# A fused gated attention and long-convolution kernel on one core: the order of all engines' tasks and their PSUM banks written out, with 81 places changed

## The chip, the core and the metric

One NeuronCore of a Trainium2 chip. Its engines run at the same time and meet through semaphores: TensorE (PE; its weight loads are shown as PEld), VectorE (DVE), ScalarE (ACT), GpSimd (POOL) and SyncE (SP). Each runs its own instructions strictly in order. SP, POOL and a little ACT issue transfers; 16 DMA engines carry them out. The metric is device microseconds of one execution; lower is better.

## The reference, cut to what matters

For each of 8 batches with S = 3136 rows:

```python
scores = (1/S) * z @ z.T                     # z: S x 64, symmetric
out    = maximum(scores, 0)**2 @ v           # v: S x 256
x      = u * out                             # S x 256
x1, x2, x3 = split(x @ w_proj, 3)            # 256 x 768
conv   = irfft(rfft(x2, axis=1) * rfft(filter))   # circular convolution over S
y      = (x1 * conv * x3) @ w_out            # float32, S x 256
```

## The kernel before, in words

**Attention.** The 3136 columns of a batch are cut into 7 chunks (512, five times, 256 and 320), the rows into tiles of 128. A unit (b, c, k) is a pair of row tiles of chunk c in batch b. TensorE computes its scores into a pair of PSUM banks (`score_mm`, matmuls that read zT_t). ACT or DVE takes the positive part into R_t (L1919 or L1921), and one of them squares it into A_t (L1928 or L1930). TensorE then weighs the rows of v with it, in two phases (matmuls that read A_t and v_t) and sums a chunk in one pair of banks. The scores are symmetric, so part of them isn't computed twice: SP issues DMA transposes of A_t into M_t, M2e_t or M2o_t (L1848), from which later chunks are weighed. A_t has 8 buffers, and a buffer is free only when its transposes have landed; M_t, M2e_t and M2o_t have one buffer each.

**From a chunk to the spectrum.** When a chunk's sum is done, DVE multiplies it with uT_t into xT_t (L1975). TensorE projects xT_t (matmuls with wp), ACT or DVE takes x1 out of PSUM (x_t), DVE multiplies it with x3 into gate_t (L1256). x2 goes through the first step of a long transform (`dft1`), is taken out as s_t and put to a scratch in HBM (spec<-s_t, L1028 and L1031). At the end of a batch eight frequency groups g = 0 to 7 follow, two to a load: SP loads spec_in_t (L1062), TensorE transforms, the result xh is multiplied with the filter's spectrum H on DVE (L1357, L1361, L1362), TensorE transforms back, the result goes to gs_t (two buffers) and back to the scratch (spec<-gs_t, L1406). Then, chunk by chunk, conv_in_t is loaded, transformed, multiplied with gate_t into yT_t (L1462), multiplied with w_out (matmuls with wo), taken out as ost_t (two buffers) and stored (out_dram<-ost_t, L1511). These steps of batch b run among the attention of batch b+1. The last batch's are split finer (`load_parts`, L1077), and three of the chunks of batch 6 are held back to fill the end, with their loads into v_t's space.

**Loads.** POOL casts u, v and z from HBM to bf16 (un_t, v_t, zn_t). DVE doubles z into zd_t (L1613), SP transposes it into zT_t (L1620), in four pieces per batch; the scores of a batch need all four. SP also transposes u into uT_t (L1565).

**The order.** The builder makes 5,477 tasks, each with an engine (or two to choose from), dependences, buffers and a cost. `Plan.go` puts them in an order by a replay on costs and then emits their instructions in this order, so it fixes each engine's queue. TensorE follows the string `ORDER`, one letter for a kind of work (S scores, w and v the two phases of a weighing, A and B and Z queues of other matmuls, Q the frequency groups), and takes within a kind the task that is ready first (`pick_pe`). ACT, DVE, SP and POOL take the ready task with the earliest start (`pick`); `ENGINES` names the engine where there is a choice. Of the four pairs of banks a task takes the one that came free first (`Pairs.take`). Where TensorE would idle near the end, `fill` puts in matmuls of the identity that keep it busy. All of this happens on the host while the program is built; on the chip an instruction waits only for what it needs and for the instructions before it on its engine.

Of the kernel before, what the change touches and what calls it, by code (L numbers as in the profile page):

```python
# [11 lines left out]
P = 128  # L12
# [10 lines left out]
INF = float("inf")  # L23
# [17 lines left out]
SPARE = 0.25  # L41
TURN = 0.235
# [14 lines left out]
    "vwSSwQwQAvAvSAvvwSAvwvSvwwwSvvQwwwSvSQvwAvQAvASvAQwwvSwvQwASAwvSwSwSvwASvSAwvAwSAvSwwwAvvASAvvAvvSSw"
    "wwSAvSAwvvSvASwAwwSBSBvwvSAvASwBvSBvAwAwABvBAwSvSwvAwAvSAvwSwwABSBwSvvAwAASAvwBvSBwAwABSwBvSvvSvvSwB"
    "ABvAwwSvwSwSAvBwABvvvSSwAwASvBvwBSwwAvSASwvwvBSBvwvASwAwwASAvQwvSQwvvSvQwwSQvwQvwQvSAvBABwAwBSAvBvvw"
    "SvSwwAASAwAvSvQwSwQwvSQvvvQwBwBwASvASwvwvSwwSvQvvwwvQSwwBvwSvBSvAvASAwASwvSSvvwQwQAvAwwvSASvSAwAQAwS"  # L60
    "wwQwSvASAvvwSwvvvSSvwvwvvwSAwSwASvwSvvAwBASBvwSwvSSwBvABvABvBwBwSBvSwvSAvwAwwSAvSAwvAwSAvBvBSvwSvAAA"
    "wABSwBwBAwwwBAAvAAvASvSvvvBABwASwwSwASAAvvSAvwvSBvSwwSwBSwSvwvSvSAvAvBQBwAvQwAvwQvwSvSQwAwwQAvvSvwQQ"
    "wwSvwAQvSAwvSwSvBwvSBvwvSAwAvvQSwBwBwQwBQvBQvvSvQwSSvwASwAvSvAwwAAwwvAvSvwwAvvwSvSAwSvwSwvBSwBAvSwAS"
    "vQSvwvvASwASwwwSQvvAwSSAwvSvwASvvSwwQwAvASAvwvvSvwwSAwASvvvwSSAvwAwAwSBABvvBwBSBwvSAvBAvSwAwASvvSBwS"
    "BvwwBwABvASvvSAwAwSSwBwBAvAASwAwBvBAAAvABSwvBSvwSvvSSvwBvBwwAwAvSSwwvvwAAAwSAvwSAvASSvwwvwSSQvvBwBQv"
    "vBSvBwwSvwAwAvwSSvAwAQvQvwSvQAwBABQwwvSvSQwBvwBAQAvSvvAQAwwAwQAvwSSvSwwvSSwAvvvSwQAvQwvSwQwwBSvQBvvS"
    "wvwwAvSvvwSvwwSAvQvwQvwSSvwSvAwSASvwAwSSAwwAwSASwvwvSSwvAwAvSAvASwwAvAvSvvSvwwvSwSvAvvAwBSBwvBwSBBBv"
    "wSvSAvAwwSSvvwSwSBvBwAvASvwwwSwBvBSAvAvvwwSwAAAAAvASwvSASwvBABSvvwSAvASwwwSwvwvvwSvSwvSSAwABvwvSwBSv"
    "wwSwSvwSBvBBvvBSvwvwASvAvwSwSAwASvAvAvSwASAwAvAQwvQwBvSwBQAwAwSvQAvwAwwQvvQvwSvQwABwBAQvwSvSQvvSwwQw"
    "BvSBvQvvSwSwwwvSvvvwwSAvSvAwwwSQvSvvSAwAvwSAvASASAQwSwwwQvSwQvASwASwvvwSwAvASvvwQSwwvAvAvSvvwSwwSABw"  # L70
    "BAvSvvSABABAwAwSSvvSvwASwASvwBSwBvwAwSAvSvAvAvSwBvwSBwAwAwAwSBABvvSAwAvSAwABSBwBvSvwBSvvvwSAvAAwABvB"
# [75 lines left out]
class Pairs:  # L147
# [5 lines left out]
    def when(self, ahead=0):  # L153
        return sorted(self.freed)[ahead]
# [1915 lines left out]
```

## Time and profile before

| what | value |
|---|---|
| three runs, median | 948.25 us (946.97 to 950.78) |
| the profiled execution, first to last instruction | 944.1 us |
| TensorE busy | 914.1 us (97%) |
| DVE, ACT, POOL busy | 838.5, 819.7, 248.8 us |
| TensorE's granted clock, mean | 0.997 |
| DMA, mean over the span | 181 GB/s |
| longest waits of TensorE by the profile | 2.1 us for gate_t, 1.8 us for v_t, 1.6 us for M_t |

The profile has one execution. Busy times are unions of the instructions' spans; a busy TensorE need not be at its peak, since the ends of matmuls are modelled. A wait is idle time of an engine just before an instruction, put down to the event that came last. SP's instructions count as issues: their length is the time for which SP was held, and the transfer lands later. Transfers of one kind are named out<-in, as M_t<-A_t.

### The profile page before, as it was taken

Reading aid. Unit: us, or ns where it says so; the run is one execution under the profiler, and the core shown is the slowest. Engines: PE = TensorE matmul, PEld = TensorE weight load, DVE = VectorE, ACT = ScalarE, POOL = GpSimd, SP = SyncE. Lnnn points to the kernel's source line nnn. Section 1 sums busy time; section 2 is a strip of 40 time slices with the busy share of each in tenths; the row PEclk is TensorE's granted clock in tenths of the full one; section 3 lists DMA queues with packets and bytes.
Section 4 is the critical chain, followed back from the end, with each engine's and each line's share of the span. In section 5 each row is a group of like instructions: output and inputs, shape, how many; then the busy total and the mean of one; then the engine's idle time right before and its main releaser. Section 6 shows DMA issues by size and latency. Waiting matters only on the chain.

```text
span 944.1 us, 30298 instructions
## 1 busy us (share of the span) xinstructions
PE 914.1 (97%) x12423; PEld 557.1 (59%) x12423; DVE 838.5 (89%) x1116; ACT 819.7 (87%) x953; POOL 248.8 (26%) x585
## 2 busy tenths in 40 slices
PE   8999999999999999999999999999999999999986
PEld 3446565566555666556665665666665666666654
DVE  8987899998888998999888988989988999899785
ACT  7968988999889988888989998889988999899573
POOL 5244223231322322223121321333123140101030
PEclk9999999999999999999999999999999999999999
DMA  9999799978999889998899989999889989897867
GB/s 155 162 181 181 117 179 184 181 150 182 170 217 201 146 181 192 209 156 159 190 183 215 176 155 200 173 184 174 183 172 207 221 138 196 193 216 132 193 189 241
DMA packets 331643, 170.70 MB, mean 181 GB/s; under 512 B 242886, under 2 KB 307142, under 8 KB 331504
## 3 DMA queue, kind: packets, MB, share of 16 engines
q1 hardware_dynamic: 301624, 131.98, 70.1%
q0 software_dynamic: 29168, 35.13, 26.4%
q8 instruction: 97, 1.59, 0.7%
q10 hardware_dynamic: 712, 1.66, 0.6%
q14 instruction: 42, 0.34, 0.1%
HBM read 90.26 MB, written 53.05 MB: 152 GB/s over the span
## 4 chain that ended last, share of the span: by engine, by line
PE 77%; DMA 10%; DVE 6%; ACT 3%; issue 2%; SPq 1%; POOL 0%; ACTq 0%; DVEq 0%; POOLq 0%
PE ps_s L516 77%; DMA M_t<-A_t 4%; DMA out_dram<-ost_t 1%; ACT R_t L1919 1%; DMA M_t<-spec_in_t 1%; DVE xh L1357 1%; ACT A_t L1928 1%; DVE yT_t L1462 1%; DVE A_t L1930 1%; DMA v_t<-spec 1%; DMA spec<-gs_t 1%; DMA M2e_t<-A_t 1%; ACT gs_t L582 1%; DVE R_t L1357 1%; DMA spec_in_t<-spec 0%
## 5 line engine op out<-in xcount | busy, mean ns | idle before, releaser
L516 PE MATMUL ps_s<-A_t,v_t 64*128 64x512 bf16 (+5 forms) x4766 | 516.1, 352 | 0.9 <-DVE A_t L1930 0.7
L516 PEld LDWEIGHTS <-v_t 64*128 64x128 bf16 (+1 forms) x6528 | 306.4, 98 | 187.7 <-PE ps_s L516 19.3
L1919 ACT ACTIVATE R_t<-ps_s 128x1024 f32<-128x1024 f32 (+3 forms) x359 | 336.9, 962 | 47.4 <-PE ps_s L516 43.8
L1928 ACT ACTIVATE A_t<-R_t 128x1024 bf16<-128x1024 f32 (+2 forms) x281 | 271.8, 993 | 15.3 <-DMA M_t<-A_t 6.3
L1930 DVE SCALAR_TENSOR_TENSOR A_t<-R_t 128x1024 bf16<-128x1024 f32 (+3 forms) x211 | 233.6, 1123 | 21.6 <-ACT R_t L1919 12.1
L516 PE MATMUL ps_s<-zT_t 64*128 64x512 bf16 (+5 forms) x1186 | 192.2, 351 | 3.6 <-DVE gate_t L1256 2.1
L1921 DVE TENSOR_SCALAR R_t<-ps_s 128x1024 f32<-128x1024 f32 (+4 forms) x153 | 170.2, 1123 | 20.9 <-PE ps_s L516 10.4
L639 POOL COPY tick<-A_t 1x1 bf16<-1x1 bf16 x159 | 56.2, 354 | 428.0 <-ACT A_t L1928 264.2
L516 PE MATMUL ps_s<-xT_t,wp 64*128 64x512 bf16 (+3 forms) x976 | 124.7, 352 | 0.1
L516 PE MATMUL ps_s<-M_t,v_t 64*128 64x512 bf16 (+4 forms) x860 | 97.2, 353 | 3.2 <-DMA M_t<-A_t 2.4
L516 PEld LDWEIGHTS <-zT_t 64*128 64x128 bf16 (+1 forms) x1219 | 69.1, 97 | 51.7 <-issue 8.2
L582 ACT ACTIVATE x_t<-ps_s 128x1024 bf16<-128x1024 f32 (+3 forms) x75 | 69.5, 928 | 22.8 <-PE ps_s L516 22.5
L1357 DVE TENSOR_TENSOR xh<-xh,H 128x1024 bf16<-128x1024 bf16 x120 | 81.7, 685 | 2.3 <-ACT xh L582 1.4
L1256 DVE TENSOR_TENSOR gate_t<-ps_s,x_t 128x512 bf16<-128x512 f32 (+2 forms) x112 | 64.4, 617 | 12.4 <-PE ps_s L516 9.0
L1462 DVE TENSOR_TENSOR yT_t<-ps_s,gate_t 128x1024 bf16<-128x1024 f32 (+2 forms) x53 | 56.9, 1078 | 14.3 <-PE ps_s L516 14.1
L1975 DVE TENSOR_TENSOR xT_t<-ps_s,uT_t 128x512 bf16<-128x512 f32 (+2 forms) x112 | 64.0, 613 | 6.3 <-PE ps_s L516 5.8
L516 PEld LDWEIGHTS <-wp 64*128 64x128 bf16 (+1 forms) x976 | 48.0, 96 | 29.7 <-PE ps_s L516 2.0
L516 PE MATMUL ps_s<-wp,xT_t 64*128 64x256 bf16 (+2 forms) x944 | 64.2, 266 | 0.8 <-ACT R_t L1919 0.7
L516 PE MATMUL ps_s<-wo,yT_t 64*128 64x256 bf16 (+2 forms) x904 | 62.1, 266 | 2.2 <-DVE yT_t L1462 1.0
L625 POOL DMA_DIRECT2D un_t<-in_u_dram x112 | 57.9, 518 | 17.4 <-issue 15.6
L651 POOL DMA_DIRECT2D v_t<-in_v_dram x112 | 58.2, 524 | 14.1 <-issue 10.4
L516 PEld LDWEIGHTS <-xT_t 64*128 64x128 bf16 (+1 forms) x944 | 44.1, 97 | 19.3 <-issue 1.5
(156 smaller groups left out, 905.7 us busy)
## 6 DMA issues: line engine op xcount, KB each, us to landing
out_dram<-ost_t SPq DMA_DIRECT2D x60, 256.0 KB
spec_in_t<-spec SPq DMA_DIRECT2D x56, 192.0 KB
spec<-gs_t SPq DMA_DIRECT2D x56, 192.0 KB
v_t<-in_v_dram POOLq DMA_DIRECT2D x80, 128.0 KB, 4.8
un_t<-in_u_dram POOLq DMA_DIRECT2D x80, 128.0 KB, 4.4
spec<-s_t SPq DMA_DIRECT2D x40, 256.0 KB
conv_in_t<-spec SPq DMA_DIRECT2D x34, 256.0 KB
out_dram<-ost_t SPq DMA_DIRECT2D x18, 128.0 KB
```

The costliest lines, as they stand in the source:

```text
L516: got = nc.tensor.matmul(o, *args, **kw)
L582: got = nc.scalar.activation(out_, in_, AF.Copy)
L625: nc.gpsimd.dma_start(out=t[ds(j * N1, N1), lo - t0 : hi - t0, :], in_=x[:, n2 : n2 + hi - lo, :])
L651: nc.gpsimd.dma_start(out=t[ds(j * N1, N1), ds(v_at(a), (b - a) * D)], in_=r[:, n2 + a - lo : n2 + b - lo, :].rearrange("p t d -> p (t d)"),)
L1256: has_read(nc.vector.tensor_tensor(o[:, :, ::-1] if h == 0 else o, p, x, ALU.mult), p)
L1357: nc.vector.tensor_tensor(x[:, 1 - i], x[:, 0], h, ALU.mult)
L1462: has_read(nc.vector.tensor_tensor(yb["y"][:, :, 0:w], p, gates[b, c][:, :, 0:w], ALU.mult), p)
L1919: has_read(nc.scalar.activation(r, p, AF.Relu), p)
L1921: has_read(nc.vector.tensor_single_scalar(r, p, 0.0, ALU.max), p)
L1928: nc.scalar.activation(a, r, AF.Square, scale=1.0 / float(S))
L1930: nc.vector.scalar_tensor_tensor(a, r, inv_s2, r, ALU.mult, ALU.mult)
L1975: has_read(nc.vector.tensor_tensor(x[:, :, ::-1] if h == 0 else x, f, ut, ALU.mult), f)
```

## The change

Before, a string of letters, a list of engines and the planner's own rules gave the order. After, the order itself is stored: `ORDER` holds two characters for each task, and `go` emits the tasks one after the other; `BANKS` holds the pair of banks of each task that takes one. Codes past the last task stand for the identity matmuls in one of the four pairs. `pick_pe`, `pick`, `offer` and the test in `fill` are gone; a task that is not ready when its turn comes makes the build fail. The tasks, their instructions, their dependences and buffers are the same, but for four tasks on another engine and for 10 identity groups in place of 12.

Against the order in which the kernel before issues, the stored one differs in 81 places, which were chosen on a replay of traced transfers. The codes can't be read by eye, so the differences that matter below are spelled out here (b is the batch; times are the starts in the profile before, to find them).

SP's queue:

| instruction | at, us | moved |
|---|---|---|
| spec<-s_t, b 3, first tiles | 374.83 | behind both M_t<-A_t that begin at 376.13 |
| spec_in_t<-spec, b 2, g 4 and 5 | 388.95 | ahead of M2e_t<-A_t (384.76) and out_dram<-ost_t (386.76); uT_t<-un_t (391.51) goes with it |
| M_t<-A_t, b 3, two of them | 399.80, 401.42 | the first directly behind the store of 386.76, then the load of 397.85, then the second, then the put of 394.55, M2o_t<-A_t of 404.64, the store of 392.89, zT_t of 407.21, spec<-s_t of 399.29 |
| out_dram<-ost_t, b 1; zT_t<-zd_t, b 4 | 416.68; 421.97 | eight and four places down |
| spec<-s_t, b 4, first tiles | 494.53 | behind both M_t<-A_t that begin at 495.41 |
| spec_in_t<-spec, b 3, g 4 and 5 | 504.18 | three places down |
| out_dram<-ost_t, b 2, last | 540.95 | nine places down |
| out_dram<-ost_t, b 3 | 617.19 | behind both M_t<-A_t that begin at 619.18 |
| zT_t<-zd_t, b 6, third piece | 624.99 | four places down, behind spec<-s_t of 633.19 |
| spec<-gs_t, b 4, first | 637.96 | ahead of the store of 633.78 and the load of 635.93 |
| spec_in_t<-spec, b 4, g 6 and 7 | 635.93 | behind M_t<-A_t of 640.81 |
| spec<-gs_t, b 4, second; zT_t<-zd_t, b 6, last piece | 643.16; 649.55 | behind the three M_t<-A_t that begin at 652.31, in this order |
| out_dram<-ost_t, b 3 | 647.47 | behind the put of 659.53 |
| spec<-gs_t, b 5, third | 760.35 | eight places down |
| spec_in_t<-spec, b 6, g 6 and 7 | 840.42 | five places down |
| spec_in_t<-spec, b 7, first half | 881.53 | behind the first two v_t<-spec (888.57, 889.13) |
| gs_t<-spec, b 7, the second pair | 886.88 | behind conv_in_t<-spec of 890.32 |

Some ten more move by one to three places. TensorE: 34 groups move by one to ten places, 16 of them in batch 0; among the others the weighing from M_t that begins at 504.81 (behind the groups at 505.24 and 505.68). Some 20 groups change places in their pair of banks; for most it follows from the move. DVE: the copy into zd_t at 620.65 moves behind the eviction xh<-ps_s at 624.78; four more tasks move by two to four places. ACT: six tasks swap with neighbours. POOL: two loads of v. A square in batch 0, one in batch 5 and an x1 eviction in batch 0 go from DVE to ACT, one positive part in batch 0 from ACT to DVE.

```diff
--- before.py
+++ after.py
 ORDER = (
-    "ASSAwSSvAwSSAwwSSvvwSBvwSvSwvSvwSwSvvSwSSvwwSvvwwSvwAvSwAwwSvSvSAvvwwSwwSvvvSABwvBwwSvvAwAvSSwwvSSwA"
...
+    "0G0H00010203130I170J1404050K1806150L190716080C1B091G0D1Crx1H0A1A0B1D1L1I1Q0E1M0O1F0F1K1R1N1V1Zry1Wrz"
...
 )
...
 ENGINES = (
...
-KINDS = {"A": "FA", "B": "FB", "Z": "FZ", "w": "W"}
+BANKS = (
+    "0123012312313213213213212301330130303102102102102021201213213131231210120210212010232132132132032032"
...
+)
+CODES = "0123456789ABCDEFGHIJKLMNOPQRSTUVWXYZabcdefghijklmnopqrstuvwxyz!#$%&()*+,-./:;<=>?@[]^_{|}~"
...
     def __init__(self, n):
         self.freed = [0.0] * n
 
-    def when(self, ahead=0):
-        return sorted(self.freed)[ahead]
-
-    def take(self, now=0.0):
-        k = min(range(len(self.freed)), key=lambda i: self.freed[i])
+    def take(self, k):
         self.freed[k] = INF
         return k
 
...
     def __init__(self):
         self.free = {e: 0.0 for e in ("PE", "ACT", "DVE", "SP", "POOL")}
         self.queues = {"S": [], "Q": [], "W": [], "FA": [], "FB": [], "FZ": []}
-        self.pend = {e: [] for e in ("ACT", "DVE", "SP", "POOL")}
         self.form = None
         self.flips = {}
...
         seen = {}
         for s in task.takes:
             k = seen.get(id(s), 0)
-            t = max(t, s.when(k))
+            t = max(t, s.freed[self.bank] if s is self.pairs else s.when(k))
             seen[id(s)] = k + 1
         return t
 
...
         return t + (a / f if a / f <= b / (1 - f) else a + b)
 
...
-        return best and (best[1], best[2], e)
-
-    def fill(self, until):
-        if self.queues["S"] or self.queues["W"] or not any(self.queues.values()):
-            return False
-        start = self.free["PE"]
-        if until < start + c_pe(512) + SPARE or self.pairs.when() > start:
-            return False
-        self.got = [(self.pairs, self.pairs.take(start))]
+
+    def fill(self, bank):
+        self.bank = bank
+        self.got = [(self.pairs, self.pairs.take(bank))]
         self.form = "H"
         self.filler()
-        self.free["PE"] = start + c_pe(512)
-        self.pairs.freed[self.got[0][1]] = self.free["PE"]
-        return True
+        self.free["PE"] += c_pe(512)
+        self.pairs.freed[bank] = self.free["PE"]
 
     def go(self):
+        every = self.tasks + [t.second for t in self.tasks if t.second]
         either = [t for t in self.tasks if t.kind is None and len(t.cost) > 1]
         assert len(either) == len(ENGINES)
         for task, e in zip(either, ENGINES):
             e = {"a": "ACT", "d": "DVE", "p": "POOL"}[e]
-            for x in task.cost:
-                if x != e and task in self.pend[x]:
-                    self.pend[x].remove(task)
             task.cost = {e: task.cost[e]}
-        while True:
-            got = []
-            x = self.pick_pe()
-            if x:
-                got.append((x[0], 0, x[1], "PE", x[2]))
-            for i, e in enumerate(self.pend):
-                x = self.pick(e)
-                if x:
-                    got.append((x[0], i + 1, x[1], e, None))
-            if not got:
-                break
-            start, _, task, e, k = min(got, key=lambda g: g[:2])
-            if self.fill(start):
+        n = len(CODES)
+        codes = [CODES.index(ORDER[i]) * n + CODES.index(ORDER[i + 1]) for i in range(0, len(ORDER), 2)]
+        kinds = [every[k].kind for k in codes if k < len(every) and every[k].kind]
+        banks = iter(BANKS)
+        at = 0
+        for k in codes:
+            if k >= len(every):
+                self.fill(k - len(every))
                 continue
-            if not k:
-                self.run(task, e, start)
-                continue
-            (self.rest if k == "v" else self.queues[KINDS.get(k, k)]).remove(task)
-            form = "F" if task.full else "Q" if k == "Q" else "H"
-            if form == "H" and self.form == "Q" and "Q" in ORDER[self.at + 1 : self.at + 1 + NEAR]:
-                form = "Q"
-            if self.form is not None and self.form != form:
-                start += FORM
-            self.form = form
-            if k in "wv":
-                flip, turned = self.flips.get(task.sum, (0, 0.0))
-                if k == "w":
-                    task.flip = flip
-                    task.second.flip = flip ^ 1
-                    self.rest.append(task.second)
-                elif flip != task.flip:
-                    start = max(start, turned + TURN)
-                self.flips[task.sum] = task.flip, start + task.cost["PE"]
-            for x in task.flips:
-                self.flips[x] = 0, start + task.cost["PE"]
-            self.at += 1
+            task = every[k]
+            (e,) = task.cost
+            assert task.end is None and not task.left
+            if self.pairs in task.takes:
+                self.bank = int(next(banks))
+            start = max(self.free[e], self.ready_at(task))
+            assert start < INF
+            if task.kind:
+                at += 1
+                form = "F" if task.full else "Q" if task.kind == "Q" else "H"
+                if form == "H" and self.form == "Q" and "Q" in kinds[at : at + NEAR]:
+                    form = "Q"
+                if self.form is not None and self.form != form:
+                    start += FORM
+                self.form = form
+                if task.sum is not None:
+                    flip, turned = self.flips.get(task.sum, (0, 0.0))
+                    if task.second:
+                        task.flip = flip
+                        task.second.flip = flip ^ 1
+                    elif flip != task.flip:
+                        start = max(start, turned + TURN)
+                    self.flips[task.sum] = task.flip, start + task.cost["PE"]
+                for x in task.flips:
+                    self.flips[x] = 0, start + task.cost["PE"]
             self.run(task, e, start)
-        left = sum(len(q) for q in self.queues.values()) + sum(len(q) for q in self.pend.values())
-        assert not left, f"{left} tasks left over"
+        assert all(t.end is not None for t in every)
 
 
 @with_exitstack
```

More of the change, by code (lines that the diff above doesn't have):

```diff
@@ L57 @@
[L57 to L71, printed above, removed]
@@ L131, in __init__, with take @@
         self.n, self.freed, self.taken = n, [], 0
-    def take(self, now=0.0):
+    def take(self, bank=None):
         self.taken += 1
@@ L151, in __init__ @@
         self.freed = [0.0] * n
-    def when(self, ahead=0):
-        return sorted(self.freed)[ahead]
-    def take(self, now=0.0):
-        k = min(range(len(self.freed)), key=lambda i: self.freed[i])
+    def take(self, k):
         self.freed[k] = INF
@@ L211, in add @@
             self.queues[kind].append(task)
-        elif not task.left:
-            self.offer(task)
-        return task
-    def offer(self, task):
-        for e in task.cost:
-            self.pend[e].append(task)
+        return task
     def ready_at(self, task):
@@ L256, in run @@
     def run(self, task, engine, start):
-        task.slots = self.got = [(s, s.take(start)) for s in task.takes]
+        task.slots = self.got = [(s, s.take(self.bank)) for s in task.takes]
         cost = task.cost[engine]
@@ L269, in run @@
         task.emit(engine)
-        for e in task.cost:
-            if task in self.pend.get(e, ()):
-                self.pend[e].remove(task)
         lat = LAT[engine] if task.lat is None else task.lat
@@ L288, in run @@
             kid.left -= 1
-            if not kid.left and kid.kind is None:
-                self.offer(kid)
-    def pick_pe(self):
-        if self.at == len(ORDER):
-            return None
-        t, k = self.free["PE"], ORDER[self.at]
-        if k == "v":
-            s = max(t, self.ready_at(self.rest[0])) if self.rest else INF
-            return (s, self.rest[0], k) if s < INF else None
-        queue = KINDS.get(k, k)
-        best, seen = None, set()
-        for task in self.queues[queue][: {"S": 1, "W": 1, "Q": 4}.get(queue, 6)]:
-            mine = {id(s) for s in task.takes[1:]} if k == "Q" else set()
-            if mine & seen:
-                continue
-            seen |= mine
-            s = max(t, self.ready_at(task))
-            if s < INF and (best is None or s < best[0] - 1e-9):
-                best = (s, task)
-        return best and (*best, k)
-    def pick(self, e):
-        t = self.free[e]
-        best = None
-        for task in self.pend[e]:
-            s = max(t, self.ready_at(task))
-            if e in task.ports:
-                s = max(s, self.port["POOL" if e == "DVE" else "DVE"])
-            key = (round(s / 0.03), task.prio, task.no) if s < INF else None
-            if key and (best is None or key < best[0]):
-                best = (key, s, task)
-        return best and (best[1], best[2], e)
-    def fill(self, until):
-        if self.queues["S"] or self.queues["W"] or not any(self.queues.values()):
-            return False
-        start = self.free["PE"]
-        if until < start + c_pe(512) + SPARE or self.pairs.when() > start:
-            return False
-        self.got = [(self.pairs, self.pairs.take(start))]
+    def fill(self, bank):
+        self.bank = bank
+        self.got = [(self.pairs, self.pairs.take(bank))]
         self.form = "H"
         self.filler()
-        self.free["PE"] = start + c_pe(512)
-        self.pairs.freed[self.got[0][1]] = self.free["PE"]
-        return True
+        self.free["PE"] += c_pe(512)
+        self.pairs.freed[bank] = self.free["PE"]
     def go(self):
+        every = self.tasks + [t.second for t in self.tasks if t.second]
         either = [t for t in self.tasks if t.kind is None and len(t.cost) > 1]
```

143 lines of the change are left out of this document (124 added, 19 removed).

## The prediction, made before the changed kernel ran

> **What bounds the kernel now.** I read the page first, then a table of stretches, then the waits and the timeline inside them.
>
> ```profile
> span 944.1 us, 30298 instructions
> PE 914.1 (97%) x12423; PEld 557.1 (59%) x12423; DVE 838.5 (89%) x1116; ACT 819.7 (87%) x953; POOL 248.8 (26%) x585
> ```
>
> TensorE is busy in 914.1 of 944.1 us, so an order that leaves its work alone can win 30.0 us at the very most. The span of 944.1 us stands against a median of 948.25 us over three runs; the 4.1 us between them lie outside the program's instructions and stay, so I take the changes from both alike. Where are the 30 us? In the table of stretches TensorE's busy time is the first number after the comma, and the last but one is the mean busy share of the 16 DMA engines:
>
> ```profile
> 25.00:275.00 250.00, 248.85 (x3082) 140.66 (x3078) 223.21 (x282) 220.39 (x249) 77.51 (x178) 1.00 1.02 171
> 375.00:425.00 50.00, 47.21 (x682) 27.34 (x679) 46.02 (x69) 43.58 (x48) 13.33 (x32) 1.00 1.10 183
> 500.00:525.00 25.00, 23.37 (x396) 13.08 (x394) 22.30 (x37) 23.04 (x25) 6.27 (x16) 1.00 1.15 210
> 600.00:675.00 75.00, 72.13 (x1084) 46.31 (x1080) 68.39 (x95) 66.76 (x78) 21.94 (x49) 1.00 1.04 174
> 885.00:901.20 16.20, 13.69 (x212) 8.24 (x208) 11.21 (x15) 4.67 (x5) 2.12 (x4) 1.00 0.93 241
> 901.20:944.14 42.94, 31.62 (x571) 20.00 (x569) 30.37 (x47) 24.66 (x47) 10.09 (x19) 0.97 0.74 214
> ```
>
> Idle TensorE: 1.15, 2.79, 1.63, 2.87, 2.51 and 11.32 us. The four stretches that begin at 375, 500, 600 and 885 us are those in which SP's order changes most; together they hold 9.80 us. The rest of the idle time lies at the start, between 275 and 300 us (where nothing is moved) and in the last 43 us. I work through the four, one by one.
>
> **A, 375 to 425 us (2.79 idle).** Rows of the timeline, with the idle time ahead of an instruction and what ended it in brackets; the two rows without an engine's operation are pieces of the chain of waits, from issue to landing.
>
> ```profile
> 374.83 0.38 SPq L1028 DMA_DIRECT2D spec<-s_t  x1
> 376.13 4.75 SPq L1848 DMA_TRANSPOSE M_t<-A_t  x2
> 383.82 1.06 ACT L1928 ACTIVATE A_t<-R_t 128x1024 bf16<-128x1024 f32 x1 [1.58 <-DMA M_t<-A_t]
> 387.70 0.41 PE L516 MATMUL ps_s<-spec_in_t,S 49*64 49x512 bf16 x4 [1.02 <-ACT xh L582]
> 388.95 2.44 SPq L1062 DMA_DIRECT2D spec_in_t<-spec  x3
> 392.89 1.55 SPq L1511 DMA_DIRECT2D out_dram<-ost_t  x2
> 394.55 3.19 SPq L1406 DMA_DIRECT2D spec<-gs_t  x3
> 397.71 0.43 PE L516 MATMUL ps_s<-spec_in_t,S 49*64 49x512 bf16 x4 [0.54 <-DMA spec_in_t<-spec]
> ...
> 393.83 5.95 DMA out_dram<-ost_t
> 399.80 7.75 DMA M_t<-A_t
> ...
> 408.65 0.63 PE L516 MATMUL ps_s<-M_t,v_t 64*64 64x512 bf16 x8 [0.75 <-DMA M_t<-A_t]
> ```
>
> A1: the load issued at 388.95 goes ahead of a transpose and a store that stood before it; the wait of 0.54 at 397.71, which is for that load, goes. A2: the M_t transpose issued at 399.80 passes the store at 392.89 and the put at 394.55, so 1.55 + 3.19 = 4.74 us of issuing no longer stand before it. Its landing is what TensorE waits for at 408.65. I take the whole 0.75; it would be 0 if the transpose's buffer came free no earlier than now. A3: the wait of 1.02 at 387.70 hangs on ACT, which had stood 1.58 us for the transposes issued from 376.13. The put at 374.83 goes behind them. SP stood idle from 375.21 to 376.13, so the transposes are not issued earlier; only the put's traffic leaves their way. Between 0 and 1.02 I take the middle, 0.5. Sum of A: 0.54 + 0.75 + 0.5 = 1.8.
>
> **B, 500 to 525 us (1.63 idle).**
>
> ```profile
> 497.44 7.33 DMA M_t<-A_t
> 504.81 0.61 PE L516 MATMUL ps_s<-M_t,v_t 64*128 64x512 bf16 x4 [1.63 <-DMA M_t<-A_t]
> 505.24 0.61 PE L516 MATMUL ps_s<-wp,xT_t 64*128 64x256 bf16 x8
> 505.68 0.61 PE L516 MATMUL ps_s<-M2o_t,v_t 64*128 64x512 bf16 x4
> ```
>
> The group that waits at 504.81 moves behind the two that start at 505.24 and 505.68. Groups start 0.43 and 0.44 apart here, so the two cover 0.87 us of the wait. A put of one tile moves behind the transposes here too, as in A3, which can take up to the other 0.76. Between 0.87 and 1.63 I take 1.2. If the landing is late all the same, the matmuls queued behind the group are those that wait now.
>
> **C, 600 to 675 us (2.87 idle).**
>
> ```profile
> 617.19 1.87 SPq L1511 DMA_DIRECT2D out_dram<-ost_t  x2
> 619.18 5.71 SPq L1848 DMA_TRANSPOSE M_t<-A_t  x2
> 620.65 0.36 DVE L1613 COPY zd_t<-zn_t 128x768 bf16<-128x768 bf16 x1 [1.66 <-DMA zn_t<-in_z_dram]
> 622.19 0.63 PE L516 MATMUL ps_s<-wo,yT_t 64*64 64x256 bf16 x16 [0.80 <-DVE x_t L586]
> 631.11 0.41 PE L516 MATMUL ps_s<-spec_in_t,S 49*64 49x512 bf16 x4 [0.54 <-ACT x_t L582]
> 633.59 0.41 PE L516 MATMUL ps_s<-xh,TZ 64*64 64x512 bf16 x4 [0.56 <-DVE xT_t L1975]
> ```
>
> The copy at 620.65 waited 1.66 us for a load of z, with DVE's evictions queued behind it. It moves four places down DVE's queue, and the wait of 0.80 at 622.19 goes (what it costs when the cover is gone: the same 0.80, later). The store of 617.19 goes behind the transposes of 619.18. The chain leads from these through ACT and DVE to the waits 0.54 and 0.56. It also leads into them from a TensorE group that reads their buffer, so they are issued no earlier; only the store's traffic leaves. Of the 1.10 I take half, 0.55, between 0 and 1.10. Sum of C: 1.35.
>
> [...]
>
> **D, 885 to 901 us (2.51 idle).**
>
> ```profile
> 881.53 2.80 SPq L1077 DMA_DIRECT2D spec_in_t<-spec  x4
> 888.57 1.58 SPq L1091 DMA_DIRECT2D v_t<-spec  x3
> 889.16 0.40 PE L516 MATMUL ps_s<-T,conv_in_t 64*128 64x128 bf16 x8 [0.22 <-DMA conv_in_t<-spec]
> 895.17 0.86 PE L516 MATMUL ps_s<-T,v_t 64*128 64x128 bf16 x16 [1.76 <-DMA v_t<-spec]
> 897.35 1.00 SPq L1077 DMA_DIRECT2D spec_in_t<-spec  x3
> 901.25 0.63 PE L516 MATMUL ps_s<-spec_in_t,S 49*64 49x256 bf16 x9
> ```
>
> One of the two loads that share the row at 881.53 goes behind the v_t loads of 888.57, and one of the gs_t loads between them too. The v_t loads come at least half of 2.80, 1.4 us, earlier, and the waits 0.22 and 1.76 can go. But the last spectrum, at 901.25, needs the load issued at 897.35 as well, which no move touches; so most of the 1.76 comes back as a wait there. What is left is the 0.22, which lies on that load's own chain, and a part of the 1.76 for DVE, which then has less in its queue when the spectrum comes. I take 0.7, between 0 and 1.98. The moved load has until 901.25; it hides.
>
> **E, the rest.** Some twenty TensorE groups move one to ten places in batches 0 to 3, where 25 to 275 us has 1.15 us to give. Three squares or evictions go from DVE to ACT and one comes back. The last 43 us only swap neighbours, and the waits there are for DVE and ACT. I take 0.3, between -0.5 and 1.0.
>
> **F, a new wait.** A put, a store and the last piece of batch 6's z go behind the three transposes at 652.31:
>
> ```profile
> 643.16 1.54 SPq L1406 DMA_DIRECT2D spec<-gs_t  x3
> 647.47 1.98 SPq L1511 DMA_DIRECT2D out_dram<-ost_t  x2
> 649.55 1.31 SPq L1620 DMA_TRANSPOSE zT_t<-zd_t  x1
> 652.31 3.76 SPq L1848 DMA_TRANSPOSE M_t<-A_t  x3
> 662.34 0.40 PE L516 MATMUL ps_s<-zT_t 64*128 64x512 bf16 x2
> ```
>
> The three end at 652.31 + 3.76 = 656.1, and without 1.54 + 1.98 + 1.31 = 4.83 us of issues before them at 651.2. Then comes the put, so z's piece is issued at 652.8. With the 7.33 of B it lands at 660.1, while its first reader comes at 662.34, or at about 658.7 with the 3.6 us won before (A, B and half of C). That is up to 1.4 us late, with the scores of a whole batch queued behind; but a single transpose should land sooner than B's two. Between 0 and 1.4 I take 0.4.
>
> **Sum.** 1.8 + 1.2 + 1.35 + 0.7 + 0.3 - 0.4 = 4.95 us: a span of 939.2 us and a median of 943.3 us.
>
> **Rivals.** (1) *The same traffic in another order.* The DMA engines' share is 0.93 to 1.15 in the four stretches, so a transfer that comes earlier delays those that it overtakes, and TensorE waits for these. Only what needs no transfer stays: B's 0.87, C's 0.80, E's 0.3, together 1.97; 946.3 us. Against it: the overtaken stores are waited for by nobody soon. The moves may also fit the one execution from which their transfers were taken, and not do on another what they say; that ends here too. (2) *Everything comes.* All 9.80 us of the four stretches go: 938.5 us. For it, that each wait there has a move beside it; against it, the load at 897.35. (3) *Slower: a transpose waits for the store in front of it.* The chain in A goes from the landing of a store (393.83 + 5.95 = 399.78) straight to the M_t transpose issued at 399.80. If that is a rule and not chance, SP stands 5.95 - 1.55 = 4.4 us, with its whole queue behind, wherever a store or put now comes directly ahead of a transpose. New such places are at about 387 (harmless: the transpose had 4.74 to give), at about 634 and at F. The last two put z's piece off to 652.8 + 8.8 = 661.6 and its landing to 668.9, 6.6 us after 662.34; it decides from the moment that z lands after its reader. Less the 1.97 of rival 1 that is 4.6 us slower: 952.9 us. Against it: at 375.21 to 376.13 SP stood 0.92 us only, right behind a put.
>
> **How the numbers follow.** Forecast 45%, rival 1 28%, rival 2 16%, rival 3 11%. The likeliest one's own range is 941.0 to 946.0. A change under 0.5% (4.7 us) can hardly be told from none here: three runs of the kernel before span 946.97 to 950.78. Faster than 943.5: two thirds of the forecast and all of rival 2, 0.46. Slower than 953.0: most of rival 3, with F's wait longer than reckoned, 0.09. The rest, 0.45. The range of 938.0 to 951.0 leaves out half of rival 2 and most of rival 3, somewhat under 2 in 10.
>
> **What would show it.** Idle TensorE in the same four stretches: near 1.0, 0.4, 1.5 and 1.8 us where 2.79, 1.63, 2.87 and 2.51 are now. A is right if no matmul that reads M_t or spec_in_t waits for its transfer there; B if the group of 504.81 waits under 0.5; C if the copy into zd_t no longer stands ahead of the evictions and the last two waits shrink; D if the wait for v_t is gone and the spectrum still starts on its late load; F by what the first score of batch 6 waits. I am wrong if the named waits are gone and others of the same size stand a few us later (rival 1), or if SP's transposes show waits for a store (rival 3).

## The result, and the profile after

The changed kernel takes 942.95 us (median of 18 runs, 937.73 to 948.38), the kernel before, run beside it, 949.1 us (18 runs, 941.8 to 957.19): a ratio of 0.9936, 95% interval 0.9912 to 0.996, or 6.1 us less. The forecast was 943.3 us. The ratios here and below leave out the few runs that took over 1.5% longer than the fastest of their kernel. Single runs of one kernel differ by more than the change is worth, so the parts below are read from the traces, stage by stage, and the times only tell whether a sum is possible at all.

The profile of the changed kernel, first lines (a line of its code is 37 lines further down than the same line before):

```profile
span 941.2 us, 30280 instructions
PE 915.3 (97%) x12415; PEld 558.9 (59%) x12415; DVE 836.7 (89%) x1116; ACT 821.7 (87%) x953; POOL 246.4 (26%) x585
```

The same stretches as in the prediction; after the comma comes TensorE's busy time, and the last three numbers are TensorE's granted clock, the DMA engines' busy share and GB/s:

```profile
25.00:275.00 250.00, 248.65 (x3074) 140.03 (x3070) 221.58 (x281) 221.06 (x249) 76.93 (x176) 1.00 1.03 171
375.00:425.00 50.00, 49.88 (x738) 30.15 (x734) 49.26 (x73) 46.95 (x53) 14.99 (x36) 1.00 0.97 182
500.00:525.00 25.00, 24.96 (x401) 14.34 (x399) 24.31 (x38) 24.76 (x29) 6.00 (x16) 1.00 1.17 194
600.00:675.00 75.00, 74.95 (x1134) 49.05 (x1131) 70.84 (x99) 71.90 (x85) 20.15 (x48) 1.00 1.04 191
885.00:901.20 16.20, 11.97 (x177) 7.08 (x173) 11.30 (x15) 7.11 (x13) 3.19 (x6) 0.79 0.64 182
901.20:941.20 40.00, 27.75 (x491) 18.04 (x482) 25.82 (x41) 19.49 (x35) 9.06 (x17) 0.92 0.72 204
```

Idle TensorE in the three middle stretches was 2.79, 1.63 and 2.87 us and is 0.12, 0.04 and 0.05 us: 7.1 us gone, more than the forecast's 4.35 for these stages. The end gives part of it back. Idle time in 885 to 901 us grew from 2.51 to 4.23 us, and the granted clock, 1.00 and 0.97 before, is 0.79 and 0.92. The stretch is the same, the work in it is not: TensorE comes to it 8.4 us ahead (884.15 for 892.56, the same group). At 884.84 us TensorE starts on v_t 10.3 us sooner than before (895.17), with no wait; the first spectrum comes 7.0 us sooner (894.23 against 901.25), and the span is only 2.9 us shorter. In the chain of waits of the changed kernel and in TensorE's timeline:

```profile
884.00 0.38 SPq L1065
884.43 6.15 DMA spec<-s_t
...
890.65 0.29 SPq L1114
890.99 4.12 DMA spec_in_t<-spec
...
894.23 0.64 PE L553 MATMUL ps_s<-spec_in_t,S 49*64 49x256 bf16 x2 [3.58 <-DMA spec_in_t<-spec]
```

The last put of s_t lands 6.15 us after it began, only then are the last loads issued, and TensorE stands 3.58 us. The granted clock (third number from the end) before, in and behind this gap, in stretches of 3 us of the same trace:

```profile
888.00:891.00 3.00, 2.52 (x48) 1.58 (x44) 2.76 (x4) 0.82 (x1) 1.06 (x2) 1.00 0.82 270
891.00:894.00 3.00, 0.00 (x0) 0.00 (x0) 1.39 (x2) 0.58 (x1) 0.00 (x0) 0.94 0.77 220
894.00:897.00 3.00, 2.48 (x17) 0.85 (x21) 1.01 (x2) 1.40 (x3) 1.06 (x2) 0.50 0.58 135
897.00:900.00 3.00, 3.00 (x45) 2.10 (x46) 2.96 (x5) 3.00 (x8) 0.00 (x0) 0.50 0.31 89
```

In the 6 us from 894 us on the granted clock is 0.50.

### The profile page after: what moved, and what is told of

The parts are those of the page before. It is cut to its first block, busy times and chain, and to the rows that moved or that the text cites. A ratio compares the mean times of both kernels' runs of the same rounds, so it can differ in the third digit from the quotient of the medians.

```text
span 941.2 us, 30280 instructions
## 1 busy us (share of the span) xinstructions
PE 915.3 (97%) x12415; PEld 558.9 (59%) x12415; DVE 836.7 (89%) x1116; ACT 821.7 (87%) x953; POOL 246.4 (26%) x585
## 3 DMA queue, kind: packets, MB, share of 16 engines
q10 hardware_dynamic: 712, 1.66, 0.6%
## 4 chain that ended last, share of the span: by engine, by line
PE 85%; DMA 4%; ACT 4%; DVE 4%; SPq 2%; issue 1%; DVEq 0%; POOL 0%; ACTq 0%; POOLq 0%
PE ps_s L553 85%; DMA spec_in_t<-spec 2%; ACT R_t L1956 1%; DVE A_t L1967 1%; DMA M2o_t<-A_t 1%; DMA spec<-s_t 1%; DVE xh L1394 1%; ACT A_t L1965 1%; DVE xT_t L2012 1%; SPq L1885 0%; DMA A_t<-spec 0%; DVE xh L623 0%; DMA spec<-uT_t 0%; ACT s_t L619 0%; DVE yT_t L1499 0%
## 5 line engine op out<-in xcount | busy, mean ns | idle before, releaser
L1965 ACT ACTIVATE A_t<-R_t 128x1024 bf16<-128x1024 f32 (+4 forms) x283 | 273.3, 992 | 9.1 <-DVE R_t L1958 4.9
L1967 DVE SCALAR_TENSOR_TENSOR A_t<-R_t 128x1024 bf16<-128x1024 f32 (+4 forms) x209 | 231.3, 1123 | 17.6 <-ACT R_t L1956 10.3
L676 POOL COPY tick<-A_t 1x1 bf16<-1x1 bf16 x159 | 53.4, 336 | 420.6 <-ACT A_t L1965 262.4
```

The source lines that it names most:

```text
L1965: nc.scalar.activation(a, r, AF.Square, scale=1.0 / float(S))
L1967: nc.vector.scalar_tensor_tensor(a, r, inv_s2, r, ALU.mult, ALU.mult)
```

## The experiments

All times are medians beside runs of the kernel before on the same chip; idle TensorE is the length of the stretch less its busy time, in one trace per kernel. The last column is the time from the issue of the last put of s_t (884.00 above) to the end of the span. Kernels built on before's order come first, those built on the changed one behind it. The runs were made on three chips: the kernel before took 949.39 us (35 runs) beside e1 to e4, 952.0 us (20) beside e5 to e8 and 948.65 us (31) beside e9 to e12. So the ratios can be compared across these groups, the medians cannot.

| kernel | us (runs) | ratio, 95% | 375-425 | 500-525 | 600-675 | put to end |
|---|---|---|---|---|---|---|
| before | 949.1 (18) | 1 | 2.79 | 1.63 | 2.87 | 51.7 |
| e1_stored, before's order | 950.18 (12) | 0.9996 (0.9962-1.0029) | 2.90 | 0.23 | 4.55 | 53.1 |
| e5_three, + 3 moves | 945.83 (8) | 0.9927 (0.9899-0.9955) | 3.82 | 1.57 | 3.14 | 58.1 |
| e9_late, + 14 moves | 944.23 (10) | 0.9984 (0.9954-1.0014) | 2.41 | 1.66 | 0.12 | 50.6 |
| e10_early, + 21 moves | 947.63 (10) | 0.9985 (0.9948-1.0022) | 1.67 | 0.65 | 1.60 | 52.9 |
| e2_sp_only, + all 35 | 944.57 (12) | 0.9955 (0.9925-0.9985) | 0.11 | 1.78 | 0.05 | 53.7 |
| changed | 942.95 (18) | 0.9936 (0.9912-0.996) | 0.12 | 0.04 | 0.05 | 57.2 |
| e11_after_again | 942.23 (10) | 0.9937 (0.99-0.9973) | 0.11 | 0.96 | 0.05 | 58.4 |
| e6_minus_three | 944.88 (11) | 0.9941 (0.9908-0.9974) | 2.12 | 0.57 | 0.05 | 55.8 |
| e4_put_first | 943.38 (12) | 0.996 (0.9931-0.9989) | 0.11 | 0.96 | 0.27 | 54.6 |
| e3_fill | 941.43 (12) | 0.9918 (0.9887-0.9949) | 0.11 | 0.42 | 0.05 | 52.8 |
| e8_fill_no_D | 942.56 (8) | 0.9911 (0.9878-0.9943) | 0.11 | 2.95 | 0.05 | 59.2 |
| e7_fill_both | 942.16 (6) | 0.9895 (0.9866-0.9925) | 0.11 | 0.06 | 0.05 | 53.6 |
| e12_fill_again | 941.05 (10) | 0.9927 (0.9889-0.9966) | 0.11 | 0.03 | 0.05 | 52.7 |

The diffs are in tasks of `ORDER`, by their two characters and by what they are, with the time in the profile before.

### e1_stored: before's order in the stored form

```diff
 the changed kernel
-ORDER, BANKS, ENGINES as stored there (5487 entries)
+ORDER, BANKS, ENGINES as the planner of the kernel before issues (5489 entries)
```

> The order and the banks of the kernel before, written out in the stored form of the changed kernel; the instructions of each engine are the same as before, one for one. Theory A (the waits belong to the order): time within 0.3% of the kernel before, and idle TensorE in the stretches 375-425, 500-525, 600-675 and 885-901 us again near 2.8, 1.6, 2.9 and 2.5 us. Theory B (the waits of the trace before belong to one execution): the same time, but at least two of the four idle times differ by more than 1 us.

The time is that of the kernel before. Its trace is a second execution of before's order:

```profile
375.00:425.00 50.00, 47.10 (x671) 25.78 (x668) 45.27 (x64) 44.48 (x49) 13.92 (x32) 1.00 1.16 197
500.00:525.00 25.00, 24.77 (x406) 14.24 (x406) 23.55 (x36) 23.82 (x27) 6.17 (x14) 1.00 1.20 218
600.00:675.00 75.00, 70.45 (x1055) 45.26 (x1052) 67.72 (x93) 64.36 (x75) 24.16 (x54) 1.00 1.07 170
```

2.90, 0.23 and 4.55 us: A is there again at its size, C is there and larger, B is nearly gone. The same order keeps its idle stages A and C, as theory A has it; but B's wait, and the size of C's, differ by more than 1 us between two executions, as theory B has it.

### e2_sp_only: SP's 35 moves alone

```diff
 ORDER of e1_stored, with the tasks of SP in the order of the changed kernel
-SP: ... Y+ R6 ay a, ...   (put, store 617.19, two M_t<-A_t)
+SP: ... Y+ ay a, R6 ...
 TensorE, ACT, DVE, POOL, BANKS, ENGINES: as before
```

> The kernel before with SP's queue in the order of the changed kernel (35 moved transfers) and nothing else of the change. Theory A (SP's order carries it): idle TensorE under 0.6 us in 375-425; 0.8 to 1.0 us in 500-525 and 600-675, where 0.87 and 0.80 us were to come from TensorE's and VectorE's moves; ratio near 0.995. Theory B (the moves on TensorE and VectorE carry it): idle above 1.2 us in 500-525 and above 2 us in 600-675, ratio 0.998 to 1.002.

```profile
375.00:425.00 50.00, 49.89 (x709) 29.09 (x706) 48.69 (x69) 47.95 (x53) 14.96 (x35) 1.00 1.07 202
500.00:525.00 25.00, 23.22 (x388) 13.42 (x390) 21.51 (x32) 21.64 (x24) 4.68 (x12) 1.00 1.20 203
600.00:675.00 75.00, 74.95 (x1124) 48.46 (x1122) 73.03 (x100) 69.35 (x79) 24.81 (x56) 1.00 1.00 180
```

SP's order alone empties A and C. In 600 to 675 us that is more than theory A asked for: 0.05 us, though the copy into zd_t stands where it stood before. B's idle time is still there (1.78 us, of which 0.8 us is the wait for M_t). The time, 0.9955, can't be told from the changed kernel's 0.9936, so what the moves on the other engines add is open.

### e5_three and e6_minus_three: three transfers moved, or all but these

```diff
 e5_three, SP's tasks of e1_stored
-D^ Jv J@ MY Ne Np N#       (store 392.89, put 394.55, ..., M_t 399.80 and 401.42, M2o_t)
+J@ MY Ne Np Jv N# D^
-R6 ay a,                   (store 617.19, M_t 619.18 and 621.44)
+ay a, R6
```

(`J@` is the load of 397.85 and `MY` the put of 399.29.) In e6_minus_three the same three are put back ahead of the transposes, in the changed kernel.

> The kernel before with three of its transfers moved on SP's queue and nothing else: the put of gs_t (394.55) and the store (392.89) behind the M_t transposes of 399.80, and the store of 617.19 behind the M_t transposes of 619.18. Theory A (a put or store ahead of a transpose costs its issuing time, so these three carry most of what 375-425 and 600-675 us gave): idle TensorE 0.6 to 2.1 in 375-425 (0.75 to 2.2 less than 2.8) and under 0.8 in 600-675 (2.9 and 4.6 in the two traces of before's order); ratio 0.996. Theory B (the traffic as a whole or the many other moves carry it): both within 0.5 us of the traces of before's order, ratio 0.999.

> The changed kernel with only those three transfers back ahead of the transposes. Theory A: idle TensorE comes back, 0.7 us or more in 375-425 and 2 us or more in 600-675, ratio 0.996 against 0.9936. Theory B: both stretches stay under 0.5 us, ratio 0.9936.

TensorE's waits of e5_three from 370 to 432 us (what ended the wait, total, times, longest), and the stretch of C:

```profile
PE ps_s L555 <- ACT xh L621: 3.0, 1, 3.0
PE ps_s L555 <- ACT ost_t L621: 0.8, 1, 0.8
600.00:675.00 75.00, 71.86 (x1079) 45.89 (x1077) 68.12 (x94) 66.51 (x77) 21.91 (x48) 1.00 1.03 174
```

and of e6_minus_three:

```profile
PE ps_s L555 <- DMA M_t<-A_t: 2.0, 1, 2.0
600.00:675.00 75.00, 74.95 (x1129) 48.27 (x1128) 70.84 (x98) 71.04 (x82) 23.13 (x53) 1.00 1.02 183
```

In A the two runs split the waits cleanly. With put and store moved alone, the wait for M_t is gone and the wait for ACT stays, 3.0 us long; with them back, the wait for M_t is back, 2.0 us, and that for ACT isn't. So A2 is the put and the store. The wait for ACT goes with the other early moves. The nearest of them is the put of 374.83 (A3), which e5_three leaves in front of its transposes; no run moves it alone. In C theory A falls on both sides: the store moved alone leaves 3.14 us, and put back it costs nothing. The time of e5_three, 0.9927, doesn't go with its trace, which comes from its slowest run; what made its other runs faster stays open. The time of e6_minus_three, 0.9941, can't be told from the changed kernel's.

### e9_late and e10_early: SP's moves behind and ahead of 600 us

```diff
 e9_late: of SP's 35 moves in e2_sp_only
-21 moves of tasks before 600 us
 14 moves of tasks behind 600 us
 e10_early: the other way round
```

> The kernel before with only those 14 of SP's 35 moves that lie behind 600 us. In 600-675 us the orders with all SP moves had 0.05 us of idle TensorE, before's order 2.9 to 4.6, and the store of 617.19 alone made no difference. Theory A (the moves inside the stretch do it, a piece of z's transposes moved from 624.99 behind a put, and others): idle under 1.0 us in 600-675. Theory B (the stretch begins with less outstanding in the DMA queues because of earlier moves): idle above 2 us, and the load of zn_t again lands 10.5 us after POOL begins to issue it. Either way 375-425 keeps 2.8 to 3.8 us, and the wait for v_t at the end is gone; ratio 0.996 to 0.998.

> The kernel before with the other 21 moves of SP, those ahead of 600 us. 375-425: idle 0.1 us, as with all of them. 600-675: theory A above 2 us, theory B under 1.0 us with zn_t landing 9.1 us after POOL begins to issue it. Ratio 0.997.

The stretches of A and C, e9_late first:

```profile
375.00:425.00 50.00, 47.59 (x678) 27.03 (x676) 45.76 (x67) 45.16 (x50) 13.27 (x30) 1.00 1.12 195
600.00:675.00 75.00, 74.88 (x1120) 48.02 (x1120) 71.67 (x99) 70.01 (x81) 23.53 (x53) 1.00 1.00 179
```

```profile
375.00:425.00 50.00, 48.33 (x693) 27.63 (x689) 47.04 (x68) 46.11 (x51) 13.34 (x31) 1.00 1.11 193
600.00:675.00 75.00, 73.40 (x1094) 47.05 (x1092) 69.47 (x98) 68.06 (x79) 22.32 (x50) 1.00 1.02 176
```

C goes with the moves inside its own stretch (0.12 against 1.60 us): theory A, though it asked for more than 2 us in e10_early, and 1.60 is also less than the 2.87 and 4.55 of before's order. The early moves or the spread of one execution take that part. DVE's wait ahead of the copy into zd_t is 0.8 us in e9_late, where it was 1.7 in both traces of before's order, and no matmul waits for it. A goes with the early moves, but not wholly: 1.67 us, one wait of 1.6 us for ACT, is left in e10_early, where eight other traces with A's moves show 0.11 or 0.12. That one execution went against the expectation. The times, 0.9984 and 0.9985, are higher than expected for both, but can't be told from e2_sp_only's 0.9955.

### e4_put_first: three loads behind the last put of s_t

```diff
 SP's tasks of the changed kernel
-rY rg p# ro k( qS pu k: p$     (v_t, v_t, spec_in_t, v_t, conv_in_t, gs_t, put of s_t, ...)
+rY rg ro pu k( p# qS k: p$
```

> The changed kernel with three loads (half of spec_in, a gs_t load and a conv_in piece) moved from before the last put of s_t to right behind it. Theory A (the put landed 6.15 us after its issue, 4.9 us in the kernel before, because these loads were still in the queues): landing within 5.0 us, the first spectrum about 1.2 us sooner, the end 1 us sooner, 0.9925. Theory B (the put's landing does not hang on them): 6 us as before, the same time within 0.2%, or a new wait for conv_in of up to 0.5 us at 889 us.

SP's queue and the first spectrum in its trace:

```profile
888.85 0.36 SPq L1067 DMA_DIRECT2D spec<-s_t  x1
...
892.88 1.86 SPq L1116 DMA_DIRECT2D spec_in_t<-spec  x2
...
899.93 1.49 PE L555 MATMUL ps_s<-spec_in_t,S 49*64 49x256 bf16 x11 [4.43 <-DMA spec_in_t<-spec]
```

The loads behind the put are issued 4.0 us after it (6.65 in the changed kernel), so the first half of theory A holds: the put lands sooner. (In the second trace of the changed kernel it is 5.6 us, so a part of the difference is the spread of executions.) But the last load then takes 7.00 us to land, by the chain of waits, in place of 4.12, with the three moved loads ahead of it; from put to spectrum it is 11.1 us, 10.2 in the changed kernel. The transfers changed places in the queue and nothing was won.

### e3_fill, e7_fill_both, e8_fill_no_D: identity matmuls in TensorE's gaps

```diff
 TensorE's tasks of the changed kernel; F is a group of two identity matmuls (0.22 us)
+12 F
 p%        (first spectrum, 894.23 after)
+6 F
 qu        (first group that reads A_t, 919.43 after)
+4 F
 q&        (second one, 921.39 after)
 e7_fill_both adds
+6 F
 06        (transposes at 8.46 us)
+3 F
 16        (group at 9.79 us)
 e8_fill_no_D: e3_fill, and on SP
-rY rg p# ro k( qS
+p# qS rY rg ro k(
```

(In e8_fill_no_D five more tasks of SP stand between p# and qS, as in the kernel before.) The added matmuls change no output.

> The changed kernel with 22 filler groups more (0.22 us each at full clock): 12 ahead of the first spectrum of the last batch (894.23 us in the trace after, TensorE idle 3.6 us before it), 6 and 4 ahead of the two waits for A_t at 919.43 and 921.39 us. Theory A (the idle time lowers the granted clock, and the low clock costs time that no transfer covers): granted clock 0.95 or more where the changed kernel has 0.79 and 0.92 (885 us to the end), and 1.5 to 3 us less than the changed kernel, a ratio to the kernel before of 0.991. Theory B (the end is set by transfers and by DVE and ACT, a slow TensorE is covered): clock up, time as the changed kernel, 0.9936. Theory C (the loads land sooner in most executions): the fillers stand in their way, up to 2.6 us longer, 0.996.

> The changed kernel with the 22 filler groups of e3_fill and 9 more in the first 10 us (6 ahead of the transposes at 8.46 us, TensorE idle 1.6 us before them, 3 ahead of the group at 9.79). Theory A (there too the idle time lowers the clock, granted 0.60 and 0.83 between 9 and 15 us, where TensorE then is busy without a break): clock 1.00 from 9 to 15 us, 1 us sooner than e3_fill, ratio 0.9905. Theory B (the first 15 us are set by loads and DVE): clock up and no time won, 0.9918.

> The kernel of e3_fill with the two loads of part D (half of spec_in, a gs_t load) back ahead of the v_t loads, where the kernel before has them. Theory A (D buys TensorE only an earlier start on work that is not in the chain to the first spectrum): the wait for v_t of 1.5 to 1.8 us is back in 885-901 us, the last put lands 0.5 to 1.2 us sooner, the first spectrum comes no later, time within 0.15% of e3_fill. Theory B (D is worth its wait): 1.5 us longer, 0.9935.

> The changed kernel once more, beside the next one on the same chip: 0.9936 as before; a second trace of the end. If the low clock of its first trace (0.79 and 0.92 granted behind 885 us) belongs to the order, it is there again, and 55 us or more pass between the issue of the last put of s_t and the end (57.2 in the first trace, 51.7 and 53.1 in the traces of before's order).

> The kernel of e7_fill_both once more on the chip of e11_after_again. If filling TensorE's idle time is worth something beyond the spread of the runs, it is 0.2 to 0.4% faster than the changed kernel beside it (0.990 against 0.9936), with 53 to 54 us between the issue of the last put of s_t and the end; if not, within 0.1%.

TensorE of e12_fill_again around the first spectrum: 24 identity matmuls fill the gap, the spectrum follows without a wait, and the clock stays at 1.00:

```profile
889.61 2.77 PE L556 MATMUL ps_s<-ident 64*128 64x512 bf16 x24
892.31 0.84 PE L556 MATMUL ps_s<-spec_in_t,S 49*64 49x256 bf16 x11
```

```profile
888.00:891.00 3.00, 2.84 (x46) 1.88 (x48) 3.00 (x5) 0.97 (x1) 1.06 (x2) 1.00 0.73 213
891.00:894.00 3.00, 3.00 (x43) 1.43 (x43) 1.38 (x3) 1.08 (x4) 1.06 (x2) 1.00 0.79 247
894.00:897.00 3.00, 2.72 (x61) 1.74 (x52) 2.97 (x6) 3.00 (x8) 0.00 (x0) 1.00 0.17 55
```

With the gap filled the granted clock did not fall there: the second trace of the changed kernel has 0.86 and 0.89 behind 885 us and 58.4 us from the put to the end, the three filled ones 1.00 up to 900 us and 52.7 to 53.6 us. Over all the traces, leaving out the last 5 us, the five in which the clock does not fall behind 885 us (before, e9_late, e10_early, e3_fill, e12_fill_again) have 50.6 to 52.9 us from the put to the end, the other nine 53.1 to 59.2; the clock is not the only thing in which they differ. The mean clock over whole runs is 0.9935 (median of 18) and 0.9925 (of 10) in the changed kernel, 0.9955, 0.9965 and 0.998 in the three filled ones. What it is worth in time is less sure. All three ratios (0.9918, 0.9895, 0.9927) are below both of the changed kernel (0.9936, 0.9937), by 0.1 to 0.4%, and on one chip e12_fill_again took 941.05 us beside 942.23 us; the intervals overlap each time, so 1 to 3 us is likely and not settled. Against the kernel before, the same fillers took 1.05% less in e7_fill_both and 0.73% less in e12_fill_again, the lowest medians beside their groups. The 0.1% between e12_fill_again and e11_after_again is less than the 0.2 to 0.4% that was expected if the fillers are worth something.

With the fillers in the first 10 us the granted clock is 1.00 from 9 to 15 us, where the changed kernel has 0.60 and 0.83; e3_fill, which has no fillers there, has 1.00 in its trace too, so what the fillers do for the clock there is not shown. The group that starts at 15.12 us in the changed kernel starts at 14.94 in e7_fill_both and 14.24 in e12_fill_again. What these 0.2 and 0.9 us are worth at the end no run separates: 0.9895 and 0.9927 lie on both sides of e3_fill's 0.9918.

e8_fill_no_D has a wait of 2.87 us for v_t again, so D does take that wait away. Its time, 0.9911, can't be told from e3_fill's 0.9918. Its trace can't serve for the put: the fillers stand behind the delayed v_t work there and put the spectrum off to 902.30 us, and the loads behind the put come 6.0 us after it, not sooner than e3_fill's 5.1.

## Why the prediction was right, and where it was not

**The base.** The prediction put 4.1 us outside the span. In every run of the changed kernel it is 1.7 to 1.9 us (943.01 and 941.2 in the profiled one). With the same 1.8 us the profiled execution of before took some 945.9 us (an estimate), 2.3 us less than the median. As changes were taken from both alike, the sum was not hurt.

**A: forecast 1.8, shown 2.7.** A1 and A2 came as said: no matmul waits for spec_in or M_t there, and the transpose that passes the put and the store is issued 6.4 us sooner (393.42 for 399.80). The term mis-sized is A3. "The transposes are not issued earlier; only the put's traffic leaves their way" failed: they are issued at 375.82 for 376.13, while TensorE was 0.7 us later there (354.09 for 353.36, the same group). Half of 1.02 was taken; the wait for ACT is 0.9 to 3.0 us in the traces without the move and nothing with it, but for e10_early. The rest of A is two waits of 0.2 us for ACT and DVE that the prediction did not list. SP's queue after:

```profile
375.82 3.02 SPq L1885 DMA_TRANSPOSE M_t<-A_t  x2
378.93 0.54 SPq L1065 DMA_DIRECT2D spec<-s_t  x1
...
393.42 1.26 SPq L1885 DMA_TRANSPOSE M_t<-A_t  x1
...
398.18 1.59 SPq L1443 DMA_DIRECT2D spec<-gs_t  x3
...
401.47 1.31 SPq L1548 DMA_DIRECT2D out_dram<-ost_t  x2
```

In e6_minus_three the wait that comes back is 2.0 us, for a transpose that took 7.11 us to land. Of what stands in front of it, the issuing of the store and the put is 1.20 and 1.43 us; for another 3.1 us SP stands until the put's data is there (by the profile 2.5 us for DVE and 0.6 for ACT):

```profile
391.74 1.20 SPq L1550 DMA_DIRECT2D out_dram<-ost_t  x2
396.03 1.43 SPq L1445 DMA_DIRECT2D spec<-gs_t  x3
...
400.19 2.08 SPq L1887 DMA_TRANSPOSE M_t<-A_t  x1
```

So A2 is worth something. But the prediction's price, the issuing time alone, is not the whole of it: the put in front also held the queue, for 3.1 us here, until its data was there.

**B: forecast 1.2, shown about 0.5.** The step that failed is the wait itself: 1.63 us was one execution's. In six traces with TensorE's order of before it is 1.63, 0.23, 1.57, 1.66, 0.65 and 1.78 (mean 1.25), in eight with the new order 0.04, 0.96, 0.57, 0.96, 0.42, 2.95, 0.06 and 0.03 (mean 0.75). The scatter is larger than the gain. The wait for M_t itself, by the profile, is 1.6, 0, 1.6, 1.7, 0 and 0.8 us in the six and gone in seven of the eight (2.7 us in e8_fill_no_D); the waits that are left there are for DVE. So the move does mostly what was said of it, on a wait that is smaller than taken.

**C: forecast 1.35, shown 2.8.** The size was off, and both named causes with it. The copy into zd_t need not move (e2_sp_only), and the store need not either, nor is it enough (e6_minus_three, e5_three). "They are issued no earlier" failed as well: the transposes come at 613.62 for 619.18, 5.6 us sooner, where TensorE is 3.7 us ahead. It is SP's moves inside the stretch, taken together, that empty it (e9_late); which of the six beside the store does it, no run separates.

**D: forecast 0.7, shown: not to be told from nothing.** Both halves were right: the wait for v_t goes, and the spectrum hangs on its late load, so that the wait comes back there. What the prediction didn't see is how long this wait is and that the granted clock is 0.50 behind it. In the first trace of the changed kernel it is 3.58 us, in the second less than half of that:

```profile
895.39 1.14 PE L553 MATMUL ps_s<-spec_in_t,S 49*64 49x256 bf16 x11 [1.65 <-DMA spec_in_t<-spec]
```

In both the clock is at 0.50 for 6 us or more (894 to 900 us in the first, 897 to 903 us in the second). The waits before it are of 3.58 and 1.65 us; in the trace of e1_stored the clock fell behind a stretch with 1.5 us of idle time:

```profile
900.00:903.00 3.00, 1.46 (x30) 0.77 (x26) 2.28 (x4) 0.57 (x1) 1.07 (x2) 0.99 1.01 264
903.00:906.00 3.00, 3.00 (x24) 1.70 (x22) 0.79 (x1) 0.55 (x1) 0.00 (x0) 0.50 0.82 293
```

In the first trace of the changed kernel a group of four matmuls of the same form (A_t and v_t) takes 1.09 us at a clock of 0.50 (11.45) and 0.60 us at 1.00 (13.20). In the trace of before the clock stayed at 1.00 behind the wait of 1.76 us for v_t. So the clock of 0.97 to 1.00 at the end of that trace, which the prediction took as given, was not a property of the order: e1_stored, in the same order, has 0.92 behind 901 us.

**E and F.** E's "the last 43 us only swap neighbours" overlooked that two evictions (937.49 and 938.30) go from ACT to DVE, so that six tasks change their engine in all and not four; no run separates its 0.3 us. F's wait did not come: the piece of z is issued at 648.36 and read at 654.80 with no idle time before it, so it landed within 6.4 us, and the assumed 7.33 was too long.

**The sum.** A 2.7, B 0.5 and C 2.8 are 6.0 us, and 6.1 were measured. That fits better than single traces allow: between 25 and 375 us alone idle TensorE is anything from 0.7 (e5_three) to 7.2 us (e2_sp_only), with no regard to the order. In the means of two traces each, the changed order issues the last put of s_t 10.2 us sooner than before's order and then loses 5.4 us up to the end. So what D, E and F come to together is not shown. The forecast of 4.95 had the right stages, was low in A and C by 2.4 us and high in B and D by up to 1.4, and it had the causes in C wrong. That its median came within 0.4 us of the measured one is in part luck.

**The rivals.** The first (same traffic, other order) falls for A and C; its clause that moves may fit one execution alone holds for B. The second (everything comes) holds for the three middle stretches and fails at the end. The third needed transposes that stand until a store has landed; in the changed kernel a transpose follows a store's issue after 0.1 us:

```profile
630.51 1.15 SPq L1548 DMA_DIRECT2D out_dram<-ost_t  x2
631.77 1.93 SPq L1885 DMA_TRANSPOSE M2e_t<-A_t  x1
```

What this rival started from may be more than chance, though. In the two other traces with before's order there (e1_stored first, then e9_late) the M_t transpose is again issued 0.02 us after the same store has landed:

```profile
400.20 5.96 DMA out_dram<-ost_t
406.18 7.81 DMA M_t<-A_t
...
397.22 5.25 DMA out_dram<-ost_t
402.49 8.14 DMA M_t<-A_t
```

SP stood idle for only 0.1 to 0.3 us ahead of it. Whether the transpose waited for the landing, so that A2 took away this wait and not issuing time alone, is open.

## What to carry to other kernels

On a queue that issues in order, put transfers that nobody soon waits for behind those that feed the next stage: each store or put of gs_t in front held the queue for its issuing, 1.15 to 3.19 us in the rows here, and one of them for as long as its data was not there (3.1 us in e6_minus_three). It need not cost time: with the store put back in C, 0.05 us of idle TensorE was left there. Before an order is fitted to a trace, take a second trace of the same order: of the three idle stages here the second trace had one at its size, one half as large again, and one nearly gone. Where a chain of transfers left TensorE idle for 3.58 and 1.65 us, the granted clock was 0.50 behind the gap; with matmuls that nobody reads in it, it was 1.00 up to 900 us in three traces. What that is worth in time was not settled here.

## What the runs showed of the hardware that was not expected

- The granted clock fell to 0.50 after 1.5 us of idle time in 900 to 903 us (e1_stored) and after waits of 1.65 us (e11_after_again) and 3.58 us (changed kernel). In e7_fill_both its mean is 0.63 in 903 to 906 us, after 0.57 and 0.90 us of idle time in the two stretches of 3 us before, with no wait longer than 0.6 us; in e3_fill, after 0.57 and 0.88 us in 900 to 903 and 903 to 906 us, it stayed at 1.00. Reckoned from the mean clock of stretches of 1 us, it stayed at 0.50 for 3.4 us (e1_stored from 902.9 us; changed kernel from 9.6 and from 920.9 us) or 6.8 us (changed kernel from 893.6 us, e11_after_again from 896.8 us). After 1.76 us in the trace of before it did not fall; what decides is open.
- Pairs of M_t transposes hold SP for very different times: 3.02 us at 375.82 and 5.57 us at 613.62 in the changed kernel.

```profile
613.62 5.57 SPq L1885 DMA_TRANSPOSE M_t<-A_t  x2
```

- The order fixes the kernel's work and not its time: 18 runs of the stored order lie between 937.73 and 948.38 us.
